# Moving K copies to ScalarE, memory sums to GpSimd, and re-spacing the projection chunks of an attention kernel

## The chip, the cores and the metric

The kernel runs on one core of a Trainium2 chip. The metric is the device time of one execution in microseconds (us); lower is better. Five engines work side by side, each on its own list of instructions in a fixed order: TensorE (PE, matrix products), VectorE (DVE), ScalarE (ACT), GpSimd (POOL) and SyncE (SP, which only issues transfers). They wait for one another through semaphores. An instruction that waits holds up everything behind it on its engine.

## The reference, cut to what matters

One sequence of 2048 rows and 640 columns is normalised and goes through two branches, whose results are multiplied:

```python
xn = layernorm(x)
# branch A: attention with a compressive memory, 32 heads of 20 columns, 4 segments of 512 rows
q, k, v = xn @ wq, xn @ wk, xn @ wv
for s in range(4):
    p     = softmax(q_s @ k_s.T * 20**-0.5 + causal_mask)
    a_dot = p @ v_s
    a_mem = (phi(q_s) @ M) / (phi(q_s) @ z + 1e-6)     # phi(t) = t + 1 if t > 0 else exp(t)
    o_s   = g * a_mem + (1 - g) * a_dot                # g = sigmoid(beta), one per head
    M, z  = M + phi(k_s).T @ v_s, z + phi(k_s).sum()
s = concat(o) @ wo
# branch B: a gated unit of width 1536
b = (sigmoid(xn @ w_gate) * (xn @ w_up)) @ w_down
return x + s * silu(b)
```

M and z are sums over the segments before the present one, so memory is read from segment 1 on, and segment n must add its share before segment n+1 reads.

## The kernel before

The four segments are worked off one after the other, each in 20 **slots** (so slot 0 to 79 in all; `NSLOT` is 20 and `R` is 20/24). A slot computes one block of attention scores: PE writes 4 x 512 columns of scores into `Sps` (L480), ACT turns all of them into exponentials `pt` in one instruction (L485), POOL blanks the part above the diagonal (L488), and one slot later PE multiplies `pt` with V into `Aps` (L505). `Sps` exists once, so the scores of a slot wait until the exponentials of the slot before are done.

Around these blocks everything else is fitted in by a small planner that runs when the program is built. Tasks with a due time (in slots) are pushed by `at(...)` or, relative to the present moment, by `later(...)`; a list `bulk` holds the products of the gated unit: 12 gate (`gp`, L392) and 12 up (`up`, L402) products and 8 down products (`yp`, L415) per segment. For each slot the planner works out a budget of PE time, runs the tasks that are due, and takes bulk products while the budget lasts. What it puts down is the order of instructions on each engine, written out by hand, as it were; nothing is reordered afterwards.

The tasks of the next segment m = n+1, run during segment n, are:

- `ln_stats` (L205) and `ln_norm` (L220): statistics on DVE, the reciprocal root `rstd` on POOL (L217, L218), the normalised rows `xn` on DVE (L225), and a transposing transfer from SP that fills one fourth of `xnT` (L235). In segment 0's own start-up the transposition is done on PE instead.
- `v_tile` (L316): 8 pieces of V, each needing one fourth of `xnT`, copied out of PSUM by ACT (L324).
- `k_chunk` (L252) and `q_chunk` (L277): 5 chunks each. A chunk is copied out of PSUM by `evacuate`: by ACT (L248) for segment 0, by DVE (L250) for the others. DVE then takes the largest absolute value of the K chunk, `kabs` (L262), or the absolute values of the Q chunk, `aq` (L287). `q_bound` (L292) combines both into a bound per row.
- `stage_out`, `relay`, `c_out`, `c_in` (L271, L241, L306, L311): SP sends K and Q to HBM and back in the layout that the scores need (`KT`, `QT`).
- `phi` (L327): DVE, ACT, DVE, in place in `k5` or `q5`; for K followed by a transposing transfer into `pkt`.
- `m_update` (L346): PE forms the segment's share `dm`, DVE masks it into `dmb` (L363) and adds it to the memory `Mbd` (L364). `mem_read` (L366) uses the memory in the next segment.

All PSUM results except `Sps` and `Aps` share three banks (`ps_d`). A product can only start when the result that had its bank has been read, by ACT (`tg` L395, `va` L324, `t` L418) or by DVE (`hT` L405, `aa` L419 and L462, the copies of K and Q).

Of the kernel before, what the change touches and what calls it, by code (L numbers as in the profile page):

```python
# [21 lines left out]
EPS = 1e-5  # L22
# [7 lines left out]
ALU = mybir.AluOpType  # L30
# [19 lines left out]
NU = len(UNITS)  # L50
NSLOT = NG // 2 * NU
WARM = 40
PASS = [0.41, 0.41, 0.41, 0.2, 0.61]
R = NSLOT / 24

# [2 lines left out]
def kernel(  # L58
# [14 lines left out]
    nc = tc.nc  # L73
# [16 lines left out]
    Ks = [dpool.tile([D, L], BF, name=f"Ks{i}") for i in range(2)]  # L90
# [9 lines left out]
    def at(time, cost, fn, *a):  # L100
        count[0] += 1
        heapq.heappush(tasks, (time, count[0], cost, fn, a))

    def later(lag, fn, *a):
        at(clock[0] + lag * R, 0.0, fn, *a)


    st = [dict() for _ in range(NSEG)]
# [45 lines left out]
    nhalf = cpool.tile([P, 2], F32, name="nhalf")  # L154
# [10 lines left out]
    KT = [cpool.tile([P, 4, L], BF, name=f"KT{i}") for i in range(3)]  # L165
# [39 lines left out]
    def ln_stats(n, p, i0=0, i1=2):  # L205
        s = st[n]
        x = s[f"x{p}"]
        if i0 == 0:
            s[f"mv{p}"] = lnp.tile([P, 2, 2], F32, name="mv")
            s[f"rstd{p}"] = lnp.tile([P, 2], F32, name="rstd")  # L210
        mv, rstd = s[f"mv{p}"], s[f"rstd{p}"]
        for i in range(i0, i1):
            bs = lnp.tile([P, 2, 6], F32, name="bs")
            nc.vector.bn_stats(bs[:, 0, :], x[:, i, 0:HB])
            nc.vector.bn_stats(bs[:, 1, :], x[:, i, HB:D])
            nc.vector.bn_aggr(mv[:, i, :], bs[:])
        nc.gpsimd.tensor_scalar(rstd[:, i0:i1], mv[:, i0:i1, 1], EPS, None, op0=ALU.add)  # L217
        nc.gpsimd.tensor_tensor(rstd[:, i0:i1], rstd[:, i0:i1], nhalf[:, i0:i1], op=ALU.pow)  # L218

    def ln_norm(n, p, i):  # L220
        s = st[n]
# [24 lines left out]
    def evacuate(n, dst, ps):  # L246
        if n == 0:
            nc.scalar.copy(dst, ps)  # L248
        else:
            nc.vector.tensor_copy(dst, ps)  # L250

    def k_chunk(n, c):  # L252
        s = st[n]
        if c == 0:
            s["k5"] = stg.tile([P, DC, L], BF, name="k5")
            s["kabs"] = stg.tile([P, DC], F32, name="kabs")
        ps = ps_d.tile([P, L], F32, name="psk", tag="d")
        for k in range(DC):
            nc.tensor.matmul(ps[:], lhsT=W["k"][:, k, c * P:(c + 1) * P], rhs=s["xnT"][:, k, :],  # L259
                             start=(k == 0), stop=(k == DC - 1))  # L260
        evacuate(n, s["k5"][:, c, :], ps[:])
        nc.vector.tensor_reduce(out=s["kabs"][:, c:c + 1], in_=s["k5"][:, c, :], axis=AX.X, op=ALU.max,  # L262
                                apply_absolute_value=True)
        if c in (2, 4) and n:
            later(0.9, stage_out, n, c // 4, Ks, KT, "k5")
        if c == DC - 1:
            s["IK"] = stg.tile([P, DC, H], BF, name="IK")
            nc.vector.tensor_tensor(s["IK"][:], nInd[:], s["kabs"][:].unsqueeze(2).to_broadcast([P, DC, H]),
                                    op=ALU.mult)
# [76 lines left out]
    def m_update(n, cs):  # L346
        s = st[n]
        dm = ps_d.tile([P, len(cs), HW * VW], F32, name="dm", tag="d")
        for i, c in enumerate(cs):
            w = (H1[c] - H0[c]) * VW  # L350
            for j in range(4):
                nc.tensor.matmul(dm[:, i, 0:w], lhsT=s["pkt"][:, j, c * P:(c + 1) * P],
                                 rhs=V[4 * (n % 2) + j][:, H0[c]:H1[c], :].rearrange("p h e -> p (h e)"),
                                 start=(j == 0), stop=(j == 3))
        for i, c in enumerate(cs):
            w = (H1[c] - H0[c]) * VW
            m = Mbd[:, c].rearrange("p h e -> p (h e)")[:, 0:w]
            bd = BD[:, c].rearrange("p h e -> p (h e)")[:, 0:w]
            if n == 0:
                nc.vector.tensor_tensor(m, dm[:, i, 0:w], bd, op=ALU.mult)  # L360
            else:
                dmb = stg.tile([P, HW * VW], BF, name="dmb", bufs=2)
                nc.vector.tensor_tensor(dmb[:, 0:w], dm[:, i, 0:w], bd, op=ALU.mult)  # L363
                nc.vector.tensor_tensor(m, m, dmb[:, 0:w], op=ALU.add)  # L364

    def mem_read(n, j, b):  # L366
        s = st[n]
# [220 lines left out]
    for n in range(NSEG):  # L588
        w = NSLOT * n
        m = n + 1  # L590
        if m < NSEG:
            lag = 0.0 if n else 0.5
            for p in range(2):
                for i in range(2):
                    at(w + R * (lag + 0.2 + 3 * p + 0.3 * i), 0.1, ln_stats, m, p, i, i + 1)
                    at(w + R * (lag + 1.2 + 3 * p + 0.3 * i), 0.1, ln_norm, m, p, i)
            for i in range(8):
                at(w + R * ((5.2 if i < 4 else 5.8) + 0.5 * i), 0.68, v_tile, m, i // 2, i % 2)
            for c in range(DC):
                at(w + R * (9.9 + 0.85 * c), 1.08, k_chunk, m, c)  # L600
                at(w + R * (14.0 + 0.8 * c), 1.08, q_chunk, m, c)
                at(w + R * (13.0 + 0.8 * c), 0.0, phi, m, "k5", c)
                at(w + R * (18.5 + 0.7 * c), 0.0, phi, m, "q5", c)
            at(w + R * (18.2), 1.12, q_bound, m)
            if m + 1 < NSEG:
                for p in range(2):
                    at(w + R * (16.1 + p), 0.0, x_load, m + 1, p)
            if n == 0:
                for c in range(DC):
                    at(R * (2.6 + 0.8 * c), 0.0, phi, 0, "k5", c)  # L610
            for i, cs in enumerate(([0, 1, 2], [3, 4])):
                at(w + R * (10.9 + 2.1 * i), 0.75 - 0.25 * i, m_update, n, cs)
        if n >= 1:
            for j in range(4):
                at(w + R * (1.1 + 0.3 * j), 0.0, o_ready, n - 1, j)
                at(w + R * (4.0 + 0.5 * j if j < 3 else 9.6), 0.0, xr_load, n - 1, j)
            for i in range(8):
                at(w + R * (5.4 + 1.1 * i), 0.68, o_proj, n - 1, i // 2, i % 2)
                at(w + R * (3.4 + 0.85 * i), 0.25, mem_read, n, i // 2, i % 2)
# [11 lines left out]
    owed = 0.0  # L631
    due, held = [], []
    for n in range(NSEG):
        st[n]["od"] = opool.tile([P, 4, D], BF, name="od")
        if n:
            bulk += [(1.09, fn, (n, f)) for f in range(FC) for fn in (gate, up)]
        bulk += [(1.64, down, (n, j, h)) for j in range(4) for h in range(2)]
        keep = 4 if n >= NSEG - 2 else 0
        for slot in range(NSLOT):
            pair, u = divmod(slot, NU)  # L640
            now = NSLOT * n + slot

            def more():
                nonlocal owed
                cost, fn, a = bulk.pop(0)
                owed -= cost
                fn(*a)

            def fill(until, share):
                nonlocal owed  # L650
                owed += budget * share
                while True:
                    if tasks and tasks[0][0] < until:
                        owed -= run_task()
                        if not (len(bulk) > keep and owed >= 0.5 * bulk[0][0]):
                            continue
                    if len(bulk) > keep and owed >= 0.5 * bulk[0][0]:
                        more()
                    elif not (tasks and tasks[0][0] < until):
                        break  # L660

            left = sum(b[0] for b in bulk[:max(len(bulk) - keep, 0)])
            fixed = [PASS[i % NU] + sum(t[2] for t in tasks if now + i - slot <= t[0] < now + i - slot + 1)
                     for i in range(slot, NSLOT)]
            level = min(fixed)
            while sum(max(level - f, 0.0) for f in fixed) < left:
                level += 0.01
            budget = max(level, fixed[0])
            owed = -PASS[u]
            pt = scores(n, pair, u)  # L670
            fill(now + 0.45, 0.45)
            for w in due:
                weigh(*w)
            due, held = held, []
            due.append((n, pair, u, UNITS[u][0][0], pt))
            if u == 2:
                held.append((n, pair, u, 1, pt))
            fill(now + 1.0, 0.55)
        while len(bulk) > keep:
            cost, fn, a = bulk.pop(0)  # L680
            owed -= cost
            fn(*a)
# [8 lines left out]
    n = NSEG - 1  # L691
# [40 lines left out]
```

## Time and profile before

| what | value |
|---|---|
| time, median of 3 runs | 349.35 us (348.18 to 350.74) |
| the profiled execution: its time / its span | 348.45 us / 346.7 us |
| PE busy | 329.0 us, 95% |
| DVE busy | 233.3 us, 67% |
| ACT busy | 229.4 us, 66% |
| POOL busy | 105.3 us, 30% |
| granted TensorE clock | 1.0 throughout |

The span runs from the first to the last instruction; the execution's own time is 1.75 us longer. A matmul's record lasts until its result has left the array, so records of neighbours overlap and a busy PE can still be held up; how far apart neighbouring groups *start* is the safer measure, and the prediction uses that. In the views below, a line of the timeline gives start, duration, engine, line, operation, what is written from what, and in square brackets the idle time before it and what ended it. A line of the waits gives who waited for whom: microseconds in total, how often, the longest. A line of the windows gives, for one stretch of time, the busy time and the count of instructions of PE, PEld (weight loads), DVE, ACT and POOL, then granted clock, share of the transfer engines and GB/s.

### The profile page before, as it was taken

What the parts mean: (1) busy time and instruction counts of PE and PEld (TensorE: products, weight loads), DVE (VectorE), ACT (ScalarE), POOL (GpSimd) and SP (SyncE); (2) the same over time, 40 slices, a digit from 0 to 9 for tenths busy, and PEclk for the clock granted to TensorE, in tenths of its full rate; (3) what the DMA queues carried; (4) which work ended last, traced back from release to release, by engine and by line L of the source; (5) the groups of instructions that cost most, each with busy time, mean ns of one, the idle gap of its engine ahead of it and who ended that gap; (6) DMA issues with size and microseconds to landing.
All of it is one profiled execution on the core that took longest, in us unless ns stands there. A gap on an engine that the chain in (4) does not pass through costs nothing.

```text
span 346.7 us, 8357 instructions
## 1 busy us (share of the span) xinstructions
PE 329.0 (95%) x3362; PEld 187.8 (54%) x3402; DVE 233.3 (67%) x581; ACT 229.4 (66%) x248; POOL 105.3 (30%) x147
## 2 busy tenths in 40 slices
PE   7999899989989999979999999998999999999995
PEld 6544355445555466544565456554456756544673
DVE  5332792679776676798856986599975587533445
ACT  3654779558796666546688666646688877776730
POOL 6920532222224422211222442222223323323214
PEclk9999999999999999999999999999999999999999
DMA  7955975455813651033740371013551431200032
GB/s 241 342 166 180 217 140 134 169 165 139 213 47 18 136 59 40 19 104 86 201 115 2 67 132 51 22 38 116 129 117 32 53 103 40 90 25 2 2 61 76
DMA packets 56581, 35.40 MB, mean 102 GB/s; under 512 B 31200, under 2 KB 56544, under 8 KB 56544
## 3 DMA queue, kind: packets, MB, share of 16 engines
q1 hardware_dynamic: 53024, 30.79, 36.4%
q10 hardware_dynamic: 3520, 4.10, 3.8%
q8 instruction: 26, 0.43, 0.5%
q14 instruction: 11, 0.09, 0.1%
HBM read 19.80 MB, written 8.00 MB: 80 GB/s over the span
## 4 chain that ended last, share of the span: by engine, by line
PE 64%; DVE 19%; DMA 7%; issue 5%; ACT 3%; SPq 2%; DVEq 0%; ACTq 0%
PE up L402 12%; PE gp L392 11%; PE yp L415 9%; PE psv L320 6%; PE Aps L505 6%; PE sp L460 5%; PE Sps L480 4%; PE psk L259 3%; PE psq L284 3%; DMA xnT<-xn 2%; DVE k L250 2%; DVE kabs L262 2%; DMA Ks<-k 2%; DMA KT<-Ks 2%; DVE hT L405 1%
## 5 line engine op out<-in xcount | busy, mean ns | idle before, releaser
L485 ACT ACTIVATE pt<-Sps 128x2048 bf16<-128x2048 f32 x80 | 150.1, 1877 | 40.7 <-PE Sps L480 38.9
L488 POOL TENSOR_SCALAR_AFFINE_SELECT pt<-pt 128x1024 bf16<-128x1024 bf16 (+1 forms) x80 | 75.7, 947 | 219.6 <-ACT pt L485 219.6
L392 PE MATMUL gp<-xnT,Wg 128*128 128x512 bf16 x224 | 58.4, 379 | 1.1 <-issue 0.3
L402 PE MATMUL up<-xnT,Wu 128*128 128x512 bf16 x228 | 58.6, 379 | 0.5
L415 PE MATMUL yp<-Wd,hT 128*128 128x320 bf16 x384 | 57.1, 299 | 0.1
L405 DVE SCALAR_TENSOR_TENSOR hT<-tg,up 128x512 bf16<-128x512 bf16 x48 | 32.7, 682 | 30.9 <-PE up L402 28.1
L505 PEld LDWEIGHTS <-pt 128*128 128x128 bf16 x1280 | 43.0, 96 | 17.4 <-DVE od L514 3.3
L505 PE MATMUL Aps<-va,pt 128*128 128x21 bf16 x1280 | 44.8, 173 | 3.0 <-DVE od L514 1.5
L395 ACT ACTIVATE tg<-gp 128x512 bf16<-128x512 f32 x48 | 28.6, 595 | 25.4 <-PE gp L392 23.9
L415 PEld LDWEIGHTS <-hT 128*128 128x128 bf16 x384 | 35.3, 97 | 15.0 <-issue 2.6
L419 DVE SCALAR_TENSOR_TENSOR aa<-t,yp 128x320 bf16<-128x320 bf16 x32 | 15.5, 484 | 26.7 <-ACT t L418 26.5
L392 PEld LDWEIGHTS <-Wg 128*128 128x128 bf16 x240 | 20.6, 97 | 23.5 <-issue 4.8
L402 PEld LDWEIGHTS <-Wu 128*128 128x128 bf16 x240 | 20.6, 97 | 23.0 <-issue 3.7
L480 PE MATMUL Sps<-QT,KT 21*128 21x128 bf16 (+3 forms) x512 | 31.7, 301 | 0.3
L320 PE MATMUL psv<-Wv,xnT 128*128 128x320 bf16 x160 | 26.2, 299 | 0.9 <-DMA xnT<-xn 0.7
L460 PE MATMUL sp<-Wo,oT 128*128 128x320 bf16 x160 | 25.8, 299 | 0.9 <-DVE dmb L363 0.9
L284 PE MATMUL psq<-xnT,Wq 128*128 128x512 bf16 x97 | 24.1, 379 | 2.6 <-DVE hT L405 1.4
L259 PE MATMUL psk<-xnT,Wk 128*128 128x512 bf16 x91 | 23.7, 379 | 2.3 <-DVE hT L405 1.8
L418 ACT ACTIVATE t<-yp 128x320 bf16<-128x320 f32 x32 | 14.0, 438 | 15.6 <-PE yp L415 15.4
L334 ACT ACTIVATE mn<-mn 128x512 bf16<-128x512 bf16 x35 | 21.7, 632 | 2.3 <-DVE mn L330 2.3
L480 PEld LDWEIGHTS <-KT 21*128 21x128 bf16 x512 | 9.0, 92 | 23.5 <-issue 21.9
L324 ACT CAST va<-psv 128x320 bf16<-128x320 f32 x32 | 13.6, 430 | 11.6 <-PE psv L320 11.4
(74 smaller groups left out, 338.1 us busy)
## 6 DMA issues: line engine op xcount, KB each, us to landing
KT<-Ks SPq DMA_DIRECT2D x32, 80.0 KB
QT<-Qs SPq DMA_DIRECT2D x32, 80.0 KB
xr<-in_A_x_dram SPq DMA_DIRECT2D x15, 160.0 KB
out_dram<-xr SPq DMA_DIRECT2D x15, 160.0 KB
xt<-in_A_x_dram SPq DMA_DIRECT2D x6, 320.0 KB
Wd<-in_B_w_down_dram ACTq DMA_DIRECT2D x1, 1920.0 KB
Ks<-k SPq DMA_DIRECT2D x4, 384.0 KB
Qs<-q SPq DMA_DIRECT2D x4, 384.0 KB
```

Source lines behind the costliest of these rows:

```text
L259: nc.tensor.matmul(ps[:], lhsT=W["k"][:, k, c * P:(c + 1) * P], rhs=s["xnT"][:, k, :], start=(k == 0), stop=(k == DC - 1))
L284: nc.tensor.matmul(ps[:], lhsT=W["q"][:, k, c * P:(c + 1) * P], rhs=s["xnT"][:, k, :], start=(k == 0), stop=(k == DC - 1))
L320: nc.tensor.matmul(ps[:], lhsT=s["xnT"][:, k, j * P:(j + 1) * P], rhs=W["v"][:, k, half * HB:(half + 1) * HB], start=(k == 0), stop=(k == ...
L392: nc.tensor.matmul(gp[:], lhsT=Wg[f // 4][:, k, fo:fo + P], rhs=s["xnT"][:, k, :], start=(k == 0), stop=(k == DC - 1))
L402: nc.tensor.matmul(ps[:], lhsT=Wu[f // 4][:, k, fo:fo + P], rhs=s["xnT"][:, k, :], start=(k == 0), stop=(k == DC - 1))
L405: nc.vector.scalar_tensor_tensor(out=h[:], in0=s["tg"][:], scalar=1.0, in1=ps[:], op0=ALU.add, op1=ALU.mult)
L415: nc.tensor.matmul(yp[:], lhsT=s["hT"][f][:, j * P:(j + 1) * P], rhs=W["d"][:, f, hs], start=(f == 0), stop=(f == FC - 1))
L460: nc.tensor.matmul(sp[:], lhsT=s["oT"][:, j, c, :], rhs=W["o"][:, c, hs], start=(c == 0), stop=(c == DC - 1))
L480: nc.tensor.matmul(Sps[:, r, c0:c0 + ncol], lhsT=kt[32 * r:32 * r + VW, gi, kb * P:(kb + 1) * P], rhs=qt[32 * r:32 * r + VW, gi, kb * P:L] ...
L485: nc.scalar.activation(pt[:], Sps[:], ACT.Exp, scale=SCALE)
L488: nc.gpsimd.affine_select(out=diag, in_=diag, compare_op=ALU.is_ge, fill=0.0, base=0, pattern=[[0, 4], [0, cnt], [1, P]], channel_multipli ...
L505: nc.tensor.matmul(A[:, qb, r, :], lhsT=pt[:, r, off:off + P], rhs=V[4 * (n % 2) + kb][:, 4 * g + r, :], start=first, stop=True, skip_grou ...
```

## The change

The change has six parts. (1) The K chunks of every segment are copied out of PSUM by ACT. (2) `kabs`, and with the last chunk `IK`, becomes a function of its own, `k_max`, which for segments 1 to 3 is put off by 0.7 of the planner's units. (3) The addition to the memory is done by POOL. (4) The two POOL instructions of `rstd` are put off by 0.6 units for segments 1 to 3. (5) The due times of V, K, Q, their `phi`, `q_bound` and `m_update` are others. (6) A floor: before a slot closes, it takes further bulk products until at least 1.2 us of PE work were put into it.

```diff
+FLOOR = 1.2
...
+        def root():
+            nc.gpsimd.tensor_scalar(rstd[:, i0:i1], mv[:, i0:i1, 1], EPS, None, op0=ALU.add)
+            nc.gpsimd.tensor_tensor(rstd[:, i0:i1], rstd[:, i0:i1], nhalf[:, i0:i1], op=ALU.pow)
+        if n == 0:
+            root()
+        else:
+            later(0.6, root)
...
-        evacuate(n, s["k5"][:, c, :], ps[:])
+        nc.scalar.copy(s["k5"][:, c, :], ps[:])
+        if c in (2, 4) and n:
+            later(0.9, stage_out, n, c // 4, Ks, KT, "k5")
+        if n:
+            later(0.7, k_max, n, c)
+        else:
+            k_max(n, c)
+
+    def k_max(n, c):
+        s = st[n]
         nc.vector.tensor_reduce(out=s["kabs"][:, c:c + 1], in_=s["k5"][:, c, :], axis=AX.X, op=ALU.max,
                                 apply_absolute_value=True)
-        if c in (2, 4) and n:
-            later(0.9, stage_out, n, c // 4, Ks, KT, "k5")
...
-                nc.vector.tensor_tensor(m, m, dmb[:, 0:w], op=ALU.add)
+                nc.gpsimd.tensor_tensor(m, m, dmb[:, 0:w], op=ALU.add)
...
             for i in range(8):
-                at(w + R * ((5.2 if i < 4 else 5.8) + 0.5 * i), 0.68, v_tile, m, i // 2, i % 2)
+                at(w + R * (lag + (3.5 + 0.6 * i if i < 4 else 6.0 + 0.55 * (i - 4))), 0.68, v_tile, m, i // 2, i % 2)
             for c in range(DC):
-                at(w + R * (9.9 + 0.85 * c), 1.08, k_chunk, m, c)
-                at(w + R * (14.0 + 0.8 * c), 1.08, q_chunk, m, c)
-                at(w + R * (13.0 + 0.8 * c), 0.0, phi, m, "k5", c)
-                at(w + R * (18.5 + 0.7 * c), 0.0, phi, m, "q5", c)
-            at(w + R * (18.2), 1.12, q_bound, m)
+                at(w + R * (8.8 + 1.0 * c), 1.08, k_chunk, m, c)
+                at(w + R * (13.8 + 1.1 * c), 1.08, q_chunk, m, c)
+                at(w + R * (12.8 + 0.85 * c), 0.0, phi, m, "k5", c)
+                at(w + R * (18.3 + 0.8 * c), 0.0, phi, m, "q5", c)
+            at(w + R * 19.2, 1.12, q_bound, m)
...
-                at(w + R * (10.9 + 2.1 * i), 0.75 - 0.25 * i, m_update, n, cs)
+                at(w + R * (10.0 + 3.2 * i), 0.75 - 0.25 * i, m_update, n, cs)
...
             fill(now + 1.0, 0.55)
+            while len(bulk) > keep and budget - owed - PASS[u] < FLOOR:
+                more()
```

Here `w` is the first slot of segment n, and `lag` is 0.5 for n = 0 and 0 after that. In slots, the first V piece moves from 4.3 to 3.3 in segment 0 and to 2.9 in segments 1 and 2; the first K chunk from 8.25 to 7.3; the last Q chunk from 14.3 to 15.2.

More of the change, by code (lines that the diff above doesn't have):

```diff
@@ L216, in ln_stats @@
             nc.vector.bn_aggr(mv[:, i, :], bs[:])
-        nc.gpsimd.tensor_scalar(rstd[:, i0:i1], mv[:, i0:i1, 1], EPS, None, op0=ALU.add)
-        nc.gpsimd.tensor_tensor(rstd[:, i0:i1], rstd[:, i0:i1], nhalf[:, i0:i1], op=ALU.pow)
+        def root():
[5 more added lines that the diff above has]
+            later(0.6, root)
     def ln_norm(n, p, i):
```

## The prediction

> **What bounds the kernel now.** First the page's busy shares: PE 95%, DVE 67%, ACT 66%, POOL 30%. PE bounds, so a change can only gain where PE waits. Its records overlap, so I read the timeline for group starts:
>
> ```profile
> 42.13 0.39 PE L480 MATMUL Sps<-QT,KT 21*128 21x512 bf16 x4
> 42.46 1.25 PE L392 MATMUL gp<-xnT,Wg 128*128 128x512 bf16 x5
> 43.55 0.35 PE L505 MATMUL Aps<-va,pt 128*128 128x21 bf16 x8
> 43.75 1.24 PE L402 MATMUL up<-xnT,Wu 128*128 128x512 bf16 x5
> 44.93 0.40 PE L480 MATMUL Sps<-QT,KT 21*128 21x128 bf16 x8
> ```
>
> This is slot 3 without a wait: scores 0.33, a gate, up, K or Q group 1.09, 8 `Aps` 0.20 (16: 0.41; 24: 0.61), and 0.09 more before the next scores. Read in the same way: V or output piece 0.69, down piece 1.64, bound 1.19, memory share 0.82 and 0.52, memory read 0.17. Priced so, slots 0 to 79 leave 11.8 us that PE lost. PE's rows in the waits name who:
>
> ```profile
> PE psk L259 <- DVE hT L405: 1.8, 2, 1.3
> PE Aps L505 <- DVE od L514: 1.5, 3, 0.6
> PE psq L284 <- DVE hT L405: 1.4, 2, 1.0
> PE Aps L505 <- POOL pt L488: 1.4, 2, 1.0
> PE psq L284 <- DVE Mbd L360: 1.0, 1, 1.0
> PE sp L460 <- DVE dmb L363: 0.9, 2, 0.4
> PE psv L320 <- DMA xnT<-xn: 0.7, 1, 0.7
> ```
>
> Mostly DVE reads PSUM late. The windows show where (slots 8-11; 16-19; 29-31; from just before 49 to the end of 51; 57-59):
>
> ```profile
> 61.22:77.47 16.25, 14.65 (x154) 7.50 (x156) 11.33 (x25) 9.11 (x7) 3.82 (x5) 1.00 0.48 160
> 92.56:105.35 12.79, 11.76 (x154) 7.69 (x154) 7.88 (x21) 11.68 (x14) 3.69 (x4) 1.00 0.32 80
> 143.66:159.16 15.50, 13.65 (x145) 7.87 (x147) 14.88 (x37) 6.75 (x5) 2.93 (x3) 1.00 0.26 86
> 225.00:239.31 14.31, 13.78 (x153) 7.79 (x153) 13.69 (x32) 6.75 (x5) 2.87 (x3) 1.00 0.21 64
> 257.41:267.36 9.95, 9.25 (x119) 6.14 (x119) 6.69 (x18) 8.87 (x11) 3.28 (x4) 1.00 0.25 52
> ```
>
> DVE is busy 14.88 of 15.50 and 13.69 of 14.31 us where the K chunks run, with ACT under half; ACT is busy 11.68 of 12.79 where two light slots follow each other.
>
> **The change, part by part.** The program order of the changed kernel is known. PE's total work is the same; start-up and slots 60 to 79 keep their order. I price stretches between slots: PE's work at the prices above, DVE's and ACT's as the mean durations of their groups times the instructions that the program order puts there.
>
> *Slots 0-7 (before 32.40 to 61.22).* Work 26.83 us in both; before lost 1.99: 1.15 in slot 2, where `Aps` waits for a mask that stands behind `rstd` on POOL, and 0.82 in slot 4 for `xnT`:
>
> ```profile
> 38.66 0.30 POOL L217 TENSOR_SCALAR rstd<-mv 128x1 f32<-128x1 f32 x1 [0.73 <-DVE mv L216]
> 39.05 0.57 POOL L218 TENSOR_TENSOR rstd<-rstd,nhalf 128x1 f32<-128x1 f32 x1
> 39.58 2.24 POOL L488 TENSOR_SCALAR_AFFINE_SELECT pt<-pt 128x1024 bf16<-128x1024 bf16 x2
> ...
> 47.16 0.85 PE L320 MATMUL psv<-Wv,xnT 128*128 128x320 bf16 x5 [0.65 <-DMA xnT<-xn]
> ```
>
> The chain of waits has that transfer, issue and length:
>
> ```profile
> 39.02 8.10 DMA xnT<-xn
> ```
>
> With `rstd` put off, slot 1's mask runs at once after its exponentials (from 35.44, 1.88 long): 1.15 us gone. But the first V piece moves from slot 4 into slot 3, behind the gate group. PE arrives there at 42.13 - 1.15 + 0.33 + 1.09 = 42.40, and its `xnT` quarter landed at 47.11, over 8 us after issue, among the loads of gate and up weights. It comes no earlier: `rstd` now follows a mask that ends at 37.32 + 1.10 = 38.42, so roots at 39.3, `xn` at 39.8, issue near 40.0 instead of 39.02. The other weight load issued at 39.62 landed at 47.08, at the same time as the transposition, so I take the landing as set by that traffic, 47.15; the bound above is the same 8.1 us from 40.0: 48.1. PE waits 4.75 (to 5.7), net **+2.8** (to +3.7). The stage's other shifts hide in it: `xn` stands before slot 1's `hT` on DVE, whose bank slot 3's gate group takes, so that group may start 0.95 late, inside the wait. Behind the wait stand `Aps`, hence `od`, hence (DVE) the next quarters' `xn`: the third issues near 51, lands within 2.9 us like its predecessor (48.70 to 51.59) at 54.0, and is used at 54.8.
>
> *Slots 8-19 (before 61.22 to 105.35, 44.13 us).* Before lost 0.59 (a K chunk takes the bank that `hT` has just got), 1.27 in slot 11, 0.29 in 14. In slot 11 DVE waited 1.7 us in `phi` for the transfer of K out (5.99 us, issued just after the 800 KB of Wo), with `Mbd` behind it. Now K goes out 0.92 slot ahead of `phi` instead of 0.41, ahead of Wo; SP's wait is now for ACT's copies. Work in 8-15 is 29.66; I leave 0.3. In 16-19 ACT decides: half a us to the first exponentials, ACT's work of three slots, the last exponentials. Before: 0.5 + 3.58 + 3.58 + 3.39 + 1.88 = 12.93 against 12.79 measured. After, slot 16 holds 1.88 exponentials, 0.57 bound's copy, 0.44 `t` and 0.63 `mn`, slot 17 a second `mn` for the copy, slot 18 a `t` less than before: 0.5 + 3.52 + 3.58 + 2.95 + 1.88 = 12.41; I take 12.5. Together 42.5: **-1.6**.
>
> *Segment 1 (105.35 to 189.21, 83.86 us; work 81.29).* Before lost 2.57: 1.39 and 0.49 in slots 31 and 30, 0.40 in 39, 0.26, 0.22. In each of segments 0 to 2 five conversions of 683 ns go to ACT, where the same one in the start-up took 585 (L248); in 1 and 2 five additions each go to POOL. In slots 29-31 DVE work falls from 15.9 to 11.0 us while PE's grows from 13.7 to 13.9: those waits go. New: in slot 36 the bound comes 0.83 us after the last Q chunk, with DVE's copy (0.68) and absolute values (0.44) to do, behind an `aa` of 0.48: 0.65. Left 0.40 + 0.22 + 0.65: **-1.3**.
>
> *Slots 40-59 (189.21 to 267.36).* Slots 40-56 took 68.20 for 65.71 of work. In 48-51 DVE falls from 20.1 to 14.1 us against 18.2 on PE. I leave 0.22, 0.45 (the same bound, slot 56) and 0.3: **-1.5**. Slots 57-59 by ACT's sum: 0.5 + 3.58 + 3.39 + 1.88 = 9.35 for 9.95: **-0.6**.
>
> *At nothing.* (a) ACT's K copies: in slot 29 the chunk is ready at 1.42, the exponentials end at 2.33, the copy at 2.92, the bank's next user comes at 3.81; cover 0.9 us. (b) The POOL addition: not in the trace; between 0.25 us (this addition on DVE, its shortest) and 1.39 (L468's 128x640 on POOL), nearest L189's 128x168 at 0.39, taken. Three follow one mask, and the third `dmb` waits for the first addition (two buffers): at worst 2 x 1.39 = 2.8 us on DVE in all, at best the 3.8 us of L364 off DVE, which the sums above have. Its reader is a segment away. (c) `k_max` late: `q_bound` needs `IK` five slots on. (d) V in slots 22 and 42: the quarters landed at 114.4 and 117.0; PE comes near 117.7 and 122. The third, now behind a mask on POOL, lands near 125.6 for 126.9. (e) Q on SP: the last `QT` part landed 5.6, 7.2 and 4.1 us before the slots 20, 40 and 60 that need it; 0.83 slot later is some 3 us. (f) The floor only spreads down products.
>
> *Sum:* 2.8 - 1.6 - 1.3 - 1.5 - 0.6 = -2.2. The profiled execution's 348.45 would be 346.3; the median of the runs is 0.9 above it, so **347.2**.
>
> One rule speaks against it: the Trainium skill, "TensorE: Matmul & The Clock Gate", Part 1, says that the array falls to half rate after an idle window of about 3.4 us, and stays there for about as long a busy one. In this trace the first 37 matmuls of 128x128 start 106 ns apart, for 3.9 us, the later ones 55 ns; but PE never idles over 1.4 us in the slots, so no row shows a fall. By the rule, slot 3's wait could add about 1.7 us to the sum, an estimate (half of 3.4); by the rows it adds nothing.
>
> **Rivals.**
> 1. *Slot 3's wait outweighs the rest.* Every us that the first quarter lands after 47.15 is a us. From 49.4 on, the gains of 5.0 are used up. At 48.1 and with a second start as slow as the first (3.9 us at 106 instead of 55 ns: 1.9) and the third quarter, whose margin is 0.8, late by 1: 347.2 + 1.0 + 1.9 + 1.0 = **351.1**, up to 353 if more quarters follow suit. For: 8.1 us under traffic, and a chain of `od`, `xn` and SP behind the waiting PE. Against: traffic ends at 47.1.
> 2. *ACT becomes the bound.* Where exponentials start over 0.9 us late, each of 15 K chunks holds its bank too long; 0.3 us each would make **351.7**. Against: ACT's work in the K slots stays at 12.3 for PE's 18.2 us (48-51). For: slots 4 (4.60 for 3.48) and 17.
> 3. *It gains more.* The first semaphore steps of the quarter's landing came at 45.1; landing then saves 2.0, and slots 16-19 at PE's 11.03 another 1.4: **343.8**; the middle 345.
> 4. *It doesn't do what it says:* DVE stays late by `hT` and `od` alone, half of the 5.0 is lost: **349.7**.
>
> **How the numbers follow.** A measurement of this kernel tells about 1% (3.5 us) from no change. Forecast (345.9 to 349.4) 0.42; rival 1 0.18, rival 2 0.08, rival 3 0.26, rival 4 0.06. Rivals 1 and 2 are half beyond 352.8. Faster by over 1%: 0.27; within: 0.57; slower: 0.16. The range from 344.3 to 352.9 leaves out the far ends of rivals 3, 1 and 2.
>
> **What will show it.** Right: PE waits for `xnT` in slot 3 for 4 to 6 us, slot 8 begins near 64, `Aps` no longer waits there for the mask; no PE wait for `hT`, `Mbd` or `dmb` over 0.5 us in slots 8-14, 28-34, 48-55; DVE busy some 14 us less, ACT 9 more. Wrong: `xnT` landing well before 47 or after 48.5; half-rate matmuls after the wait; K copies on ACT that PE waits for; slots 16-19 at 13 us or more.

## The result, and the profile after

The changed kernel takes 350.97 us (median of 20 executions), the kernel before 349.06 us beside it: a ratio of 1.0053, 95% interval 1.0038 to 1.0068. It is slower by half a per cent. The forecast was 347.2 us, a little faster; the sign was wrong, and the time is that of rival 1 (351.1 us).

The table has the stretches of the prediction, each from the start of its first slot to the start of the next stretch's first.

| slots | before, us | after, us | forecast of the difference | measured |
|---|---|---|---|---|
| 0-7 | 28.82 | 33.84 | +2.8 | +5.0 |
| 8-15 | 31.34 | 30.81 | -1.4 | -0.5 |
| 16-19 | 12.79 | 12.03 | -0.3 | -0.8 |
| 20-39 | 83.87 | 83.16 | -1.3 | -0.7 |
| 40-56 | 68.19 | 67.59 | -1.5 | -0.6 |
| 57-59 | 9.95 | 9.79 | -0.6 | -0.2 |
| 60-79 | 79.38 | 79.39 | 0 | 0 |

So slots 8 to 59 give 2.8 us back where 5.0 were forecast, and slots 0 to 7 cost 5.0 where 2.8 were. From the page of the changed kernel, busy times and the clock by fortieths of the span:

```profile
PE 330.2 (95%) x3360; PEld 188.7 (54%) x3402; DVE 221.7 (64%) x556; ACT 237.1 (68%) x263; POOL 110.2 (32%) x157
...
PEclk9999969999999999999999999999999999999999
```

DVE has lost 11.6 us of work (some 14 were forecast) and ACT got 7.7 (9); the 6 in the clock's row was not there before. The timeline of PE in slot 3 of the changed kernel:

```profile
41.39 1.24 PE L406 MATMUL gp<-xnT,Wg 128*128 128x512 bf16 x5
47.88 1.52 PE L334 MATMUL psv<-Wv,xnT 128*128 128x320 bf16 x5 [5.25 <-DMA xnT<-xn]
49.19 0.42 PE L519 MATMUL Aps<-va,pt 128*128 128x21 bf16 x8
49.45 2.10 PE L416 MATMUL up<-xnT,Wu 128*128 128x512 bf16 x5
51.39 0.84 PE L334 MATMUL psv<-Wv,xnT 128*128 128x320 bf16 x5
```

The wait is the one that was forecast (4.75 to 5.7 us). But after it the groups are slow as well: from one start to the next the V piece takes 1.31 us and the up group 1.94, against the prices 0.69 and 1.09. The windows of the same kernel, cut in steps of 3.41 us, have the reason in the third column from the right, the granted clock:

```profile
41.00:44.41 3.41, 1.63 (x10) 0.54 (x9) 3.31 (x10) 2.52 (x3) 0.77 (x2) 1.00 1.13 243
44.41:47.82 3.41, 0.00 (x0) 0.00 (x0) 1.23 (x4) 0.36 (x1) 2.30 (x5) 0.50 1.28 122
47.82:51.23 3.41, 3.35 (x18) 1.68 (x19) 1.42 (x5) 0.95 (x2) 0.00 (x0) 0.50 0.16 35
51.23:54.64 3.41, 3.41 (x40) 1.91 (x39) 2.23 (x6) 2.37 (x3) 0.02 (x1) 1.00 0.22 43
```

The clock fell at 44.41, inside the wait, and rose at 51.23: PE works its first 3.35 us after the wait at half clock. The chain of waits of the changed kernel (start, length, engine, what is written) has the transfer behind the wait, and one that was forecast to be hidden (slot 25):

```profile
38.78 0.57 POOL rstd L221
39.86 7.97 DMA xnT<-xn
...
126.67 4.49 DMA xnT<-xn
```

PE's rows in its waits, without those that name no other engine and the start-up's:

```profile
PE psv L334 <- DMA xnT<-xn: 5.7, 2, 5.2
PE Aps L519 <- DVE od L528: 2.9, 5, 1.0
PE Aps L519 <- POOL pt L502: 0.7, 2, 0.5
PE gp L406 <- DVE hT L419: 0.4, 1, 0.4
```

The rows of before for `psk`, `psq` and `sp` behind `hT`, `Mbd` and `dmb` are gone, as forecast. The row of `Aps` behind `od` has grown from 1.5 to 2.9 us; no step of the prediction has that. The windows answer to those of before: slots 8-11, 16-19, 29-31, 49-51, 57-59. The same slots do not hold the same work in both kernels, and the window of before for 49-51 begins 1.25 us ahead of slot 49 (226.25), so these lines are for the share that each engine is busy; times are compared in the table above.

```profile
66.27:81.75 15.48, 15.30 (x157) 7.94 (x160) 9.15 (x23) 11.64 (x12) 4.09 (x5) 1.00 0.70 222
97.08:109.11 12.03, 11.36 (x147) 6.99 (x148) 7.55 (x24) 11.62 (x14) 3.06 (x4) 1.00 0.30 82
147.38:161.61 14.23, 13.93 (x139) 7.32 (x140) 9.91 (x24) 8.89 (x9) 4.24 (x7) 1.00 0.30 97
229.49:243.72 14.23, 13.93 (x140) 7.32 (x142) 11.13 (x26) 8.29 (x8) 4.24 (x6) 1.00 0.29 92
259.87:269.66 9.79, 9.26 (x118) 6.04 (x118) 5.46 (x15) 8.69 (x11) 3.22 (x4) 1.00 0.18 54
```

DVE, full in slots 29-31 before (14.88 of 15.50 us), now has 4.3 us free there, and these three slots took 14.23 us with 13.93 us of PE in them. That DVE is freed there is shown; what frees it is taken up with e5 below.

### The profile page after: what moved, and what is told of

Same layout as the page of the kernel before. It is cut to its first block, busy times and chain, and to the rows that moved or that the text cites. A ratio compares the mean times of both kernels' runs of the same rounds, so it can differ in the third digit from the quotient of the medians.

```text
span 349.0 us, 8371 instructions
## 1 busy us (share of the span) xinstructions
PE 330.2 (95%) x3360; PEld 188.7 (54%) x3402; DVE 221.7 (64%) x556; ACT 237.1 (68%) x263; POOL 110.2 (32%) x157
## 4 chain that ended last, share of the span: by engine, by line
PE 77%; ACT 6%; DVE 5%; issue 5%; DMA 4%; POOL 2%; ACTq 0%; POOLq 0%
PE up L416 14%; PE gp L406 13%; PE yp L429 10%; PE Aps L519 8%; PE psk L266 6%; PE Sps L494 6%; PE sp L474 6%; PE psv L334 6%; PE psq L298 5%; ACT pt L499 4%; DMA xnT<-xn 4%; PE wps L543 2%; PE dm L366 1%; PE am L388 1%; ACT mn L348 1%
## 5 line engine op out<-in xcount | busy, mean ns | idle before, releaser
L416 PE MATMUL up<-xnT,Wu 128*128 128x512 bf16 x229 | 59.9, 384 | 0.5
L409 ACT ACTIVATE tg<-gp 128x512 bf16<-128x512 f32 x48 | 28.5, 595 | 22.0 <-PE gp L406 18.3
L334 PE MATMUL psv<-Wv,xnT 128*128 128x320 bf16 x160 | 27.2, 304 | 5.9 <-DMA xnT<-xn 5.7
L494 PE MATMUL Sps<-QT,KT 21*128 21x128 bf16 (+3 forms) x512 | 31.7, 301 | 0.1
L476 DVE SCALAR_TENSOR_TENSOR aa<-aa,sp 128x320 bf16<-128x320 bf16 x32 | 15.5, 485 | 16.4 <-PE sp L474 16.4
```

The lines of the kernel that those rows point to most:

```text
L334: nc.tensor.matmul(ps[:], lhsT=s["xnT"][:, k, j * P:(j + 1) * P], rhs=W["v"][:, k, half * HB:(half + 1) * HB], start=(k == 0), stop=(k == ...
L416: nc.tensor.matmul(ps[:], lhsT=Wu[f // 4][:, k, fo:fo + P], rhs=s["xnT"][:, k, :], start=(k == 0), stop=(k == DC - 1))
L494: nc.tensor.matmul(Sps[:, r, c0:c0 + ncol], lhsT=kt[32 * r:32 * r + VW, gi, kb * P:(kb + 1) * P], rhs=qt[32 * r:32 * r + VW, gi, kb * P:L] ...
```

## The experiments

All were timed in five rounds, in three groups (e1 to e4, e5 to e8, e9 to e12), each beside the kernel before on the same chip; its medians there were 348.34, 349.01 and 349.82 us, so ratios are to be compared, not times. "0-59" is the time from the start of slot 0 to that of slot 60 in the profiled execution; start-up and slots 60 to 79 hold the same work in all but e8, where some `phi` of Q runs after slot 59. The ratios are those of the measurement, with its interval, not quotients of the medians shown. In e10 to e12 some 1.8 us of PE's work lies after slot 7 instead of before it, so there only the last column compares.

| run | median, us | ratio to before, 95% | slots 0-7 | 8-59 | 0-59 |
|---|---|---|---|---|---|
| before | | 1 | 28.8 | 206.1 | 235.0 |
| changed kernel | 350.97 | 1.0053 (1.0038 to 1.0068) | 33.8 | 203.4 | 237.2 |
| e1_v_old_seg0 | 345.89 | 0.9916 (0.9883 to 0.9949) | 28.1 | 203.2 | 231.2 |
| e2_before_v_early | 353.79 | 1.0139 (1.0102 to 1.0175) | 33.7 | 205.6 | 239.3 |
| e3_keep_warm | 349.35 | 1.0024 (1.0001 to 1.0047) | 32.3 | 202.8 | 235.2 |
| e4_loads_after | 348.83 | 1.0000 (0.9976 to 1.0025) | 31.7 | 203.0 | 234.7 |
| e5_k_on_dve | 348.06 | 0.9958 (0.9927 to 0.9990) | 32.3 | 203.0 | 235.3 |
| e6_add_on_dve | 346.15 | 0.9925 (0.9897 to 0.9953) | 28.2 | 203.5 | 231.7 |
| e7_k_on_act_alone | 345.92 | 0.9894 (0.9863 to 0.9925) | 29.6 | 202.0 | 231.6 |
| e8_phi_q_later | 347.89 | 0.9972 (0.9941 to 1.0002) | 28.5 | 203.5 | 232.0 |
| e9_act_root | 348.14 | 0.9934 (0.9894 to 0.9973) | | | |
| e10_act_root_v | 346.11 | 0.9885 (0.9840 to 0.9931) | 27.7 | 204.3 | 232.0 |
| e11_spread | 351.88 | 1.0058 (1.0031 to 1.0084) | 27.2 | 210.5 | 237.7 |
| e12_q_spread | 346.49 | 0.9898 (0.9858 to 0.9937) | 27.2 | 205.1 | 232.4 |

(The profiled execution of e9_act_root took 375.4 us, 25 us and more above ten of its eleven others, so its stretches are left out.)

### The V pieces of segment 0

**e1_v_old_seg0** is the changed kernel with the old due times of V in segment 0 alone; **e2_before_v_early** is the kernel before with the new ones there, and the root of the norm put off in that segment.

```diff
 # e1, in the changed kernel; e2 has the two branches the other way round, in the kernel before
-at(w + R * (lag + (3.5 + 0.6 * i if i < 4 else 6.0 + 0.55 * (i - 4))), 0.68, v_tile, ...)
+if n == 0:
+    at(w + R * ((5.2 if i < 4 else 5.8) + 0.5 * i), 0.68, v_tile, ...)
+else:
+    at(w + R * (lag + (3.5 + 0.6 * i if i < 4 else 6.0 + 0.55 * (i - 4))), 0.68, v_tile, ...)
```

> The changed kernel with the V pieces of segment 0 alone back at their old due times (first piece in slot 4). Theory (the loss sits in slot 3's wait and the half-rate stretch behind it, and the other parts gain 2.7 us): the wait for xnT shrinks from 5.4 to about 2.5 us, no half-rate stretch, slots 0 to 7 take about 29.4 us instead of 33.9, time about 346.6. Rival (the loss comes from the work moved to ScalarE and GpSimd, the wait takes the place of others): 350 or more.

> The kernel before with only two parts of the change, and these in segment 0 alone: V pieces at the new due times and the root on GpSimd put off. Theory: the same wait of about 5.4 us in slot 3 and the same half-rate stretch, slots 0 to 7 at about 33.9 us instead of 28.8, time about 354. Rival: without the other parts of the change the wait stays under 3 us, time under 351.

Both came out by the theory that the V pieces are the loss. e1 takes slots 0-7 from 33.8 to 28.1 us and is the first version that beats both kernels; its wait is shorter than the 2.5 us expected, since the load landed early in its trace (45.86, see the table below), so its profile shows a good case:

```profile
47.26 0.85 PE L334 MATMUL psv<-Wv,xnT 128*128 128x320 bf16 x5 [0.35 <-DMA xnT<-xn]
```

And e2 adds 4.9 us to slots 0-7 of the kernel before (33.70 against 28.82), where the whole change adds 5.0, with PE's wait and a stretch at half clock, and takes 0.5 off the rest.

### The half clock by itself

**e3_keep_warm** is the changed kernel with 95 products of 128x128 that nothing reads, in the place where PE waits in slot 3.

```diff
 for i in range(8):
+    # n == 0: before the first piece
+    at(w + R * (lag + 3.5) - 0.001, 0.0, warm, 95)
     at(w + R * (lag + (3.5 + 0.6 * i ...)), 0.68, v_tile, m, i // 2, i % 2)
```

> The changed kernel with 95 matmuls of 128x128 on constants, whose result nobody reads, put in front of slot 3's first V piece: 95 x 55 ns = 5.2 us of array work inside the wait. Theory: V still starts near 47.9, but the groups behind it run at full rate; slot 3 falls by 1.5 us (0.6 V, 0.8 up, 0.1 Aps), time about 349.5. Rival (the slow groups have another cause, the transfers or a port): no change, 351.0.

The timeline of PE in e3:

```profile
42.44 5.47 PE L543 MATMUL wps<-ident 128*128 128x128 bf16 x95
47.74 0.84 PE L334 MATMUL psv<-Wv,xnT 128*128 128x320 bf16 x5
48.42 0.35 PE L519 MATMUL Aps<-va,pt 128*128 128x21 bf16 x8
48.63 1.24 PE L416 MATMUL up<-xnT,Wu 128*128 128x512 bf16 x5
49.71 0.84 PE L334 MATMUL psv<-Wv,xnT 128*128 128x320 bf16 x5
```

V starts hardly earlier than in the changed kernel (47.74 against 47.88; in this trace the quarter had landed at 46.95, and V stood behind the 95 products), yet it takes 0.68 us and up 1.08: full clock. Slots 0-7 are 1.5 us shorter (32.32), 0.1 of it the earlier start. So of the 5.0 us that these slots lost, some 1.4 to 1.5 are the clock; the other 3.5 are the wait, net of what slots 2 and 4 gained, by subtraction. The ratios, 1.0024 for 1.0053, say 1.0 us, with intervals that overlap a little.

### What the transposition waits for

**e4_loads_after** is the changed kernel with the loads of the third block of gate and up weights in slots 3 and 4 instead of 1 and 2.

```diff
-at(1.8, 0, load_glu, 2, 0)
-at(2.6, 0, load_glu, 2, 1)
+at(3.4, 0, load_glu, 2, 0)
+at(4.2, 0, load_glu, 2, 1)
```

> The changed kernel with the loads of the third block of gate and up weights (1280 KB) issued in slots 3 and 4 instead of 1 and 2, behind the transposition of the first quarter. Theory (that traffic makes the transposition take 8.0 us): it lands within 3 us of its issue near 40, PE waits under 1 us in slot 3, no half-rate stretch, slots 0 to 7 near 28 us, time about 345. Rival (the transposition is slow by itself, or behind the relays of K and Q): landing near 47, time 350 or more.

The mechanism is right: with no load ahead of it, the quarter landed 2.67 us after its issue (39.89 to 42.56) instead of 7.97, and slot 3 has no wait. The gain is not there, because the loads now stand ahead of the third quarter, issued at 48.07 and landed at 53.36. The timeline of PE in e4, and its window with the clock:

```profile
53.41 1.23 PE L334 MATMUL psv<-Wv,xnT 128*128 128x320 bf16 x5 [2.04 <-DMA xnT<-xn]
54.43 0.62 PE L519 MATMUL Aps<-va,pt 128*128 128x21 bf16 x16
54.90 2.29 PE L406 MATMUL gp<-xnT,Wg 128*128 128x512 bf16 x5
```

```profile
50.33:53.74 3.41, 1.37 (x8) 0.55 (x7) 1.67 (x5) 2.29 (x2) 0.68 (x1) 1.00 1.48 205
53.74:57.16 3.42, 3.42 (x26) 1.67 (x25) 1.26 (x4) 0.95 (x2) 0.00 (x0) 0.50 0.42 86
```

The same kind of loss, a wait (2.04 us) and the half clock, in slot 5 instead of slot 3. What is late is whichever transposition is issued just after a weight load.

The traces of all runs tell more exactly how late. The semaphore steps of the last weight load (`Wu`, issued from ACT) and of the first quarter (in the last row the third), in us:

| run | `Wu` issued | `xnT` issued | `Wu` landed | `xnT` landed |
|---|---|---|---|---|
| before | 39.62 | 39.02 | 47.08 | 47.11 |
| changed kernel | 39.64 | 39.86 | 46.52 | 47.83 |
| e1 | 40.62 | 40.85 | 45.86 | 47.21 |
| e7 | 40.09 | 40.19 | 47.10 | 48.35 |
| e10 | 40.55 | 40.91 | 47.96 | 49.22 |
| e12 | 40.39 | 40.62 | 45.32 | 46.67 |
| e4, third quarter | 47.34 | 48.07 | 52.83 | 53.36 |

Where the first quarter is issued 0.1 to 0.65 us after the load, it lands 1.25 to 1.35 us after the load has, in these five traces and in those of e2, e3, e5, e6, e8 and e11. e4's third quarter, issued 0.73 us after the load, landed 0.53 after it. Where the quarter is issued ahead (before), the two land together. The landing is thus neither a fixed time nor a fixed length after the issue: it follows the load, and the load's own 4.9 to 7.5 us differ from trace to trace.

### Which part of the change gains

**e5_k_on_dve** and **e6_add_on_dve** are e1 with one part undone (e5 for segments 1 to 3); **e7_k_on_act_alone** is the kernel before with one part done.

```diff
 # e5 (in e1)
-nc.scalar.copy(s["k5"][:, c, :], ps[:])
+evacuate(n, s["k5"][:, c, :], ps[:])
 # e6 (in e1)
-nc.gpsimd.tensor_tensor(m, m, dmb[:, 0:w], op=ALU.add)
+nc.vector.tensor_tensor(m, m, dmb[:, 0:w], op=ALU.add)
 # e7 (in the kernel before)
-evacuate(n, s["k5"][:, c, :], ps[:])
+nc.scalar.copy(s["k5"][:, c, :], ps[:])
```

> The changed kernel with segment 0's V projection at its old due times (the run e1_v_old_seg0, 345.9 us beside 348.3 before), and in it the copies of the K chunks of segments 1 to 3 back on the engine that the helper chose before (VectorE). Theory (VectorE is late where K chunks run, and the copies on ScalarE are what gains): TensorE's waits for hT, Mbd and dmb return in slots 8-14, 28-34 and 48-55; slots 8-19, 20-39 and 40-56 take together 2 to 3 us more than in e1_v_old_seg0 (193.4 us), the time near 348.5. Rival (the wider spread of K, V and Q chunks is what gains, the engine of the copy doesn't matter): within 0.5 us of e1_v_old_seg0, near 345.9.

> The run e1_v_old_seg0 with the memory's ten additions on VectorE instead of GpSimd. Theory (they are worth their 3.8 us of VectorE where VectorE is late): 0.3 to 1 us longer than e1_v_old_seg0, near 346.5, with more wait for dmb or od. Rival (the additions cost nothing on either engine, or block GpSimd's masks there): no change, 345.9, or 0.3 less.

> The kernel before with one edit: the K chunks' copies of segments 1 to 3 on ScalarE. Theory (that edit carries the gain): TensorE's waits for hT in slots 30, 31 and 48 to 54 shrink, 1.5 to 3 us less than before, near 346. Rival (in the old order of chunks it brings nothing, since three parts of the change only work together): 348.3, within 0.5 us.

e5 went against the theory. With the copies back on DVE, slots 8-59 take 203.0 us, as in e1 (203.2; the 0.2 are the third quarter of `xnT` in slot 25), and no wait for `hT`, `Mbd` or `dmb` has come back. One wait for such a copy there is, 0.39 us of a V piece in slot 7. Its windows for slots 29-31 and 49-51:

```profile
145.42:159.65 14.23, 13.93 (x139) 7.32 (x140) 12.26 (x27) 7.34 (x6) 4.23 (x7) 1.00 0.29 96
227.53:241.75 14.22, 13.92 (x139) 7.32 (x140) 13.29 (x29) 6.75 (x5) 4.23 (x6) 1.00 0.29 93
```

The same 14.23 and 14.22 us as in the changed kernel, though DVE is busy for 12.26 and 13.29 of them: the chunks lie far enough apart for DVE to follow. e7 shows the other half: with the old order and the copies on ACT, slots 8-59 take 202.0 us, 4.1 less than before. PE's rows in its waits:

```profile
PE Aps L505 <- DVE od L514: 1.5, 3, 0.6
PE psk L259 <- DVE hT L405: 1.0, 2, 0.5
PE psq L284 <- DVE hT L405: 0.5, 1, 0.5
```

`psk` and `psq` still wait for `hT`, but 1.5 us instead of 3.2, and `Aps` for `od` only 1.5 us. So in these slots the copies alone gain 4.1 us, the change without them 206.1 - 203.0 = 3.1, and both together no more than that (3.0 in e1, 2.8 in the changed kernel): they cure the same waits, and the change brings waits of its own. The 3.1 belong to all that e5 keeps, the new due times, the later `kabs` and roots, the additions on POOL and the floor; only the additions were tried by themselves. e6 is 0.37 us longer in slots 8-59 than e1, but of that 0.20 is the third quarter of `xnT` in slot 25, and only 0.07 each are `od` in slots 29 and 49. Its size is in the theory's 0.3 to 1, its cause is not: the engine of the additions hardly matters here.

The median of e5 (348.06) says something else than its slots 8-59, because its slots 0-7 do. Its twelve executions fall into two groups: five at 345.1 to 346.4 us with a mean granted clock of 0.997 or more, seven at 347.8 to 349.7 with 0.993 to 0.995. The profiled one is of the second group; its timeline of PE in slot 4:

```profile
44.67 1.25 PE L406 MATMUL gp<-xnT,Wg 128*128 128x512 bf16 x5
48.69 0.95 PE L334 MATMUL psv<-Wv,xnT 128*128 128x320 bf16 x5 [2.77 <-DMA xnT<-xn]
```

The quarter landed at 48.65 there, against 47.21 in the trace of e1. e6, e8 and e9 split in the same way (medians of the two groups 345.8 and 348.5, 346.6 and 349.5, 345.8 and 349.8), and of e1's six executions one is at 0.994. The times fit a load that lands late in some executions, with a longer wait and a half clock behind it when V stands in slot 4. Only one execution of each kernel has a trace, so for the others this is not shown. In the changed kernel, with V in slot 3, all twenty are at 0.989 to 0.995. In the group at full clock e1 and e5 are equal (345.8 and 345.6, beside 348.3 and 349.0 of the kernel before), so the verdict on e5 stands in the times too.

### The wait of `Aps` for `od`

`Aps` exists once. Its next user starts when DVE has read it into `od`, so everything that stands ahead of `od` on DVE counts. **e8_phi_q_later** is e1 with the feature maps of Q later.

```diff
-at(w + R * (18.3 + 0.8 * c), 0.0, phi, m, "q5", c)
+at(w + R * (19.7 + 0.8 * c), 0.0, phi, m, "q5", c)
```

> The run e1_v_old_seg0 with the feature maps phi of Q due at 19.7 units instead of 18.3, so that in slots 35 and 55 od stands ahead of phi on VectorE. Theory (TensorE's 0.71 us in each of slots 36 and 56 is Aps waiting for od, which stands behind phi, and not the bound that the prediction named): both go, about 1.4 us less, near 344.5; the 1.15 us of slot 14 stay. Rival (the bound or its copy holds these slots): both stay at 0.6 to 0.8, 345.9.

The timeline of slot 36 of the changed kernel, PE and then DVE, shows what was in doubt:

```profile
177.16 1.25 PE L310 MATMUL cps<-aq,IK 128*32 128x512 bf16 x5
179.05 0.57 PE L519 MATMUL Aps<-va,pt 128*128 128x21 bf16 x16 [0.64 <-DVE od L528]
```

```profile
176.04 0.49 DVE L433 SCALAR_TENSOR_TENSOR aa<-t,yp 128x320 bf16<-128x320 bf16 x1 [1.88 <-ACT t L432]
176.55 0.69 DVE L257 CAST q<-psq 128x512 bf16<-128x512 f32 x1
177.27 0.29 DVE L301 TENSOR_SCALAR aq<-q 128x512 uint16<-128x512 uint16 x1
177.48 0.29 DVE L344 TENSOR_SCALAR mn<-q 128x512 bf16<-128x512 bf16 x1
177.80 0.29 DVE L345 TENSOR_SCALAR q<-q 128x512 bf16<-128x512 bf16 x1
...
178.50 0.49 DVE L528 TENSOR_TENSOR od<-Aps,rd 128x320 bf16<-128x320 f32 x1
```

The bound `cps` starts at once behind the scores; PE is stopped by `od`, which stands behind the copy of Q, `aq` and a `phi`. In e8 the `phi` is out of the way and the loss in slots 36 and 56 falls from 0.71 to 0.18 us each, as the theory has it. But the sum doesn't fall: the `phi` now stands ahead of `od` in slots 19, 39 and 59, where the loss grows from 0.14, 0.40 and 0.40 to 0.98, 0.93 and 1.15, and slots 8-59 take 203.5 us instead of 203.2. Slots 60-79 take 79.86 us instead of 79.38: in slot 61 the scores wait 0.42 us for exponentials that `phi`'s own had held up on ACT. The theory was right on the cause and wrong on the gain; the wait moved to the next slot in which DVE is late.

### In search of a better version

**e9_act_root** is e7 with the root put off as in the change. **e10_act_root_v** is e9 with segment 0's V in slot 5. **e11_spread** is e10 with the change's due times of K, Q, `phi` and the bound; **e12_q_spread** takes of these only Q's, its `phi`'s and the bound's.

```diff
 # e10, in segment 0 (in e9)
-at(w + R * ((5.2 if i < 4 else 5.8) + 0.5 * i), 0.68, v_tile, ...)
+at(w + R * ((6.2 if i < 4 else 6.3) + 0.5 * i), 0.68, v_tile, ...)
```

> The kernel before with two edits: the K chunks' copies on ScalarE (the run e7_k_on_act_alone, 345.9 us) and the root of the norm put off by 0.6 slot. Theory (slot 2's wait of Aps for the mask behind the root, 1.55 us in e7_k_on_act_alone, goes): slots 0 to 7 in 28.0 to 28.5 us instead of 29.58, the time near 344.6. Rival (the later root only moves the quarter of xnT later, and slot 4 waits for it instead): slots 0 to 7 near 29.5, near 345.9, with executions in which the clock halves.

> The run e9_act_root with segment 0's V projection later: its first piece in slot 5 instead of slot 4. Theory (TensorE reaches the piece after the quarter has landed, so that neither the wait nor the half clock can come): slots 0 to 7 near 27.3 us, no execution with a mean granted clock under 0.996, the time near 344. Rival (the other quarters, or K behind V, are late in their turn): slots 0 to 19 no shorter than in e9_act_root.

> The run e10_act_root_v with the changed kernel's due times of the K and Q chunks, of phi and of the bound. Theory (with the copies on ScalarE the wider spread costs, by waits of Aps for od in slots 14, 36 and 56): slots 8 to 59 take 1 to 1.5 us more than in e10_act_root_v, near 345.2. Rival (V in slots 22 and 42, the additions or the floor cost those 1.1 us): no more than 0.3 us between the two.

> The run e10_act_root_v with the changed kernel's due times of the Q chunks, their phi and the bound alone, K's as before. Theory (Q's last chunk and the bound in slots 15, 16 and 36, 56 put their copies before od): the waits of slots 14, 36 and 56 are as in e11_spread, the time too. Rival (K's chunks make them): as e10_act_root_v, near 344.

e9 splits: six executions at 345.5 to 346.9 us, four at 349.4 to 350.0 with a mean clock of 0.990 to 0.994; the other two, of 375.4 and 634.3 us, belong to neither. By the times both theory and rival came, each in part of the executions; which waits they had, this run's trace can't show. e10 has no execution under 0.997, so its theory on the clock holds. The 27.7 us of its slots 0-7 are less of a gain than they look: one V piece and one gate or up group (1.8 us) now come after slot 7, PE still loses some 2.4 us in these slots (to `od` in slot 4, and to exponentials that the scores wait for in slots 4 and 6), and `Aps` costs 1.07 us by `od` in slot 9, so that 0-59 is 232.0 us for e7's 231.6. It missed 344 us, but at a ratio of 0.9885 it is the lowest of all; e7 (0.9894), e12 (0.9898), e1 (0.9916) and e6 (0.9925) lie within its interval and are not to be told from it.

e11 missed by far, for a reason that no theory had. The timelines of PE and of ACT in its slot 8:

```profile
60.30 0.85 PE L326 MATMUL psv<-Wv,xnT 128*128 128x320 bf16 x5
63.81 2.29 PE L265 MATMUL psk<-xnT,Wk 128*128 128x512 bf16 x5 [2.66 <-ACT k L267]
```

```profile
58.98 0.42 ACT L330 CAST va<-psv 128x320 bf16<-128x320 f32 x1
63.17 0.59 ACT L267 CAST k<-psk 128x512 bf16<-128x512 f32 x1 [3.77 <-issue]
```

`k5` exists once. The copy of the first K chunk must wait until the transposing transfer of segment 0's K has read it; the last of these was issued at 55.32 and landed at 63.03. ACT stood, PE behind it, and the clock halved at 63.53. (The view names no releaser for ACT's wait; that it is this transfer is read from the program and from the landing, 0.14 us ahead of the copy.) The transfer was late in the way of slot 3's: `Wd`, 1920 KB, was issued ahead of it at 54.39 and landed at 63.21, so here the transposition landed 0.2 us before the load (in e10 and e12, in the same order, 0.4 and 0.5) and not after it. e12 shares e11's 0.71 us in slots 16, 36 and 56, so these come with the places of Q and the bound; slot 14's loss it doesn't have; there a down product stands ahead of the Q chunk. Its theory is half right, its time is its rival's.

## Why the prediction was wrong, point by point

Of some 4.5 us between the forecast for the profiled execution (346.3) and the one of the changed kernel (350.85), 2.2 are in slots 0-7, points 1 and 2, and 2.2 are gains of slots 8-59 that did not come, points 3 to 6.

1. **Slots 0-7, the wait: mis-sized by 0.7 us.** Arrival (42.4) and issue (near 40.0, measured 39.86) were right. The step that failed is "I take the landing as set by that traffic, 47.15": the trace of before had the quarter issued ahead of the `Wu` load; with `rstd` later it is issued behind it, and then lands 1.3 us after it (47.83). The other bound, 48.1, was the nearer one, in part by luck: this trace's load landed at 46.52, earlier than the 47.08 of before. That the change moves an issue past another queue's load was in the numbers (39.62 and 40.0), and was not used.
2. **Slots 0-7, the clock: 1.5 us left out.** "By the rows it adds nothing" failed. No row of before had PE waiting for longer than 1.4 us, so the rows could not speak for or against; a cost that the trace cannot show was put at its lower end. The Trainium skill, "TensorE: Matmul & The Clock Gate", Part 1, was right that such a wait is followed by half rate, and the estimate from it (1.7 us) was near the 1.5 that e3 measures.
3. **Slots 8-15: the new wait for `od` in slot 14, 1.15 us where 0.3 was left for the whole stretch.** The sums of DVE's work per stretch said that it had room, which was true (22.59 of 30.81 us); the order of one slot, with a `phi` and a Q chunk's copy and `aq` ahead of `od`, says who waits. The timeline of DVE in slot 14 of the changed kernel:

```profile
88.89 0.42 DVE L352 TENSOR_TENSOR k<-k,mn 128x512 bf16<-128x512 bf16 x1
89.22 0.68 DVE L257 CAST q<-psq 128x512 bf16<-128x512 f32 x1
...
90.64 0.49 DVE L528 TENSOR_TENSOR od<-Aps,rd 128x320 bf16<-128x320 f32 x1
```

4. **Slots 16-19: better than forecast,** 12.03 for 12.5 (the sum given as 12.41 is 12.43). The sum by ACT is no lower bound there: the changed kernel was 0.4 us shorter.
5. **Slots 20-39 and 40-56: 0.7 and 0.6 for 1.3 and 1.5.** The 0.65 and 0.45 us that were laid on the bound in slots 36 and 56 were 0.71 each, and it was `od`, behind just the copy and the absolute values that the prediction named and a `phi`. Left out were `od` in slots 29 and 49 (0.3 each), 0.2 in slot 54, `hT` in slot 44 (0.4) and item (d): counted from the start of slot 20, the third quarter was forecast to land at 20.3 us (125.6 on the time scale of before, where slot 20 starts at 105.35) for a piece at 21.6; it was issued at 17.56, 1.0 us later than before, which fits, but landed at 22.05 (131.16) and cost some 0.5 in slot 25. Fifteen of its sixteen semaphore steps had come by 129.23; what held the last one is not shown.
6. **Slots 57-59: 9.79 for 9.35,** since ACT's sum took no account of `pt` from POOL (0.35 us in slot 57) and `od` (0.40 in slot 59).
7. **The claim behind the gains was half right.** The waits for `hT`, `Mbd` and `dmb` went as forecast, DVE is busy 11.6 us less and ACT 7.7 more. But that the copies on ACT make the gain, given the new order, fell with e5. Of the terms at nothing, an addition on POOL took 0.48 us where 0.39 was taken, and DVE waited 0.7 us for them in all.
8. **The rivals.** Rival 1's mechanism is what happened, with its parts of nearly the right size (landing 48.1 for 47.83, half clock 1.9 for 1.5, a late quarter 1.0 for 0.5). That its time, 351.1, is met by 350.97 is in part luck: these parts measured 2.7 of its 3.9 us, and waits that it does not have made up for the rest. They are rival 4's: DVE stays late by `od`, and 2.2 of the 5.0 us of gains were lost, slot 25's 0.5 among them. Rival 2 did not come in the changed kernel.

## What to carry to other kernels

When an edit moves the issue of a transfer past a big load on another queue, take its landing from the load's landing (here between 0.5 us before and 1.35 us after it), not from the old length, and let the reader stand later than that by the load's spread. A wait of PE of 2 us and more is priced as the wait and a half clock that may stand behind it. Two edits that cure the same wait were worth no more than one here, and before an order is widened, the result tile that exists once (`Aps`, `k5` here) should be followed through the queue of the engine that frees it.

## What was not expected of the hardware

The clock's fall needs no full idle window. The half clock lasts 3.413 us in e2, e4, e5 and e11 and twice that in the changed kernel. Cut in steps of 3.413 us, counted from the clock's first rise (in the kernel before at 5.44 us; the 1.0 of its table holds from there on), every fall and rise in the traces of the changed kernel, e2, e4, e5 and e11 lies on a step. A step in which PE was busy for 1.63 us (changed kernel, 41.00 to 44.41), 1.37 (e4) or 0.64 (e5, 45.91 to 49.32) was followed by the half clock, though PE never idled for over 2.8 us in the last two. Steps with 1.74 us (e4, near its end) and 1.99 us (e2) were not. The windows of e2:

```profile
41.24:44.65 3.41, 1.99 (x12) 0.55 (x9) 3.34 (x9) 2.35 (x3) 1.07 (x1) 1.00 1.00 224
44.65:48.06 3.41, 0.00 (x0) 0.00 (x0) 1.56 (x6) 0.72 (x2) 2.36 (x5) 1.00 1.41 168
48.06:51.47 3.41, 2.95 (x17) 1.56 (x18) 1.12 (x4) 0.95 (x2) 0.00 (x0) 0.50 0.23 47
```

So in these runs the limit lies between 1.63 and 1.74 of 3.41 us, near half. By that, where the steps fall against a wait of 2 to 3 us would decide whether it costs a half clock; no trace has such a wait in the slots without one, so this is not shown. The executions of one kernel that lie 3 us apart fit a late landing and a half clock together, but that too is argued from their times and mean clocks alone. The Trainium skill, "TensorE: Matmul & The Clock Gate", Part 1, says that a free-running window of 3.4 us decides, which these steps agree with, and calls the window idle, which here was one busy for up to 1.63 us.

A transposing transfer of the same size took 2.67 us with no weight load in flight (e4, first quarter) and 5.29 to 8.35 us when issued just behind one of 640 KB (5.29 is e4's third quarter, 8.35 e5's first).
